# A three-stage kernel: last stage's first chunks converted inside the stage before, a reordered start, and a reordered last block

## The chip, the cores and the metric

The kernel runs on one core of a Trainium2 chip, in one launch. The metric is the device time of an execution in microseconds (us); the document compares medians over runs and reads single profiled executions. The engines are TensorE (PE; its weight loads are PEld), VectorE (DVE), ScalarE (ACT), GpSimd (POOL) and SyncE (SP), which here mainly issues the transfers (DMA).

## What is computed

Three functions are applied one after the other: attention with a decay taken from a running sum, a mixture of experts with one expert per token (MoE1), and a dense layer pair with h·cos(h) between (MoE2).

```python
# attention: q, k, v (4, 8, 576, 64), s (4, 8, 576)
cum = np.cumsum(np.maximum(s, 0.0), axis=-1)
bias = -(cum[:, :, :, None] - cum[:, :, None, :])
scores = np.where(causal, -1e9, scale * q @ k.T + np.minimum(bias, 0.0))
attn = softmax(scores); x = attn @ v              # x: 2304 tokens x 512
# MoE1: 8 experts, w1 (8, 512, 1024), w2 (8, 1024, 512)
expert_idx = argmax(xn @ en.T / tau)              # xn, en: rows over their norms
out[mask] = gate_w[mask, None] * (np.maximum(x[mask] @ w1[e], 0.0) @ w2[e])
# MoE2: w_in (512, 2048), w_out (2048, 512)
h = x @ w_in
return (h * np.cos(h)) @ w_out
```

## The kernel before

**Attention** goes through 16 pairs of heads. For a pair, `load` fetches q and k, `load_c` the running sums, `load_v` the values. A pair has four steps n: `sco` makes score products on PE, `mx` adds the decay and takes the maximum on DVE, `ex` exponentiates on ACT, `tr` transposes on PE, `av` makes the products with v. The running sums `cum` are made by a scan on DVE over 32 rows (one per head), stored to DRAM as `cumd` by a transfer that ACT issues, and fetched from there, spread over partitions, as `c_t`. For the first pair there is no time for that round trip: `first_c` makes `c_t` by products of a selecting matrix (`sel2`, or a column of the identity `idt`) with `cum`, with 32 rows, copies halves of 288 columns out with ACT and DVE, and `mask` adds the causal mask on DVE and POOL. `setup_b` to `setup_d` make the norms of the expert embeddings: one product (`n_ps`), a root on POOL in some ten small operations (`en`), its inverse on DVE (`ien`). A plan (`at(pair, where, ...)`) says at which point of which pair they stand. In attention the order on all engines is written out by hand.

**MoE1** has 72 steps (`NS`), 8 for each of nine rounds of tokens. A step makes `h_ps` (12 products, `emit_h`), takes relu and splits the result into a high part `hh` (ACT) and a rest `hl` (DVE), and, one step later, adds 12 products to four accumulators (`emit_o`). Every matrix is held as a high part and a rest, so that each product is three (high·high, high·rest, rest·high). After a round's eighth step the four accumulators become `x2h` (ACT copy) and `x2l` (DVE subtraction), the input of MoE2. `finish` writes the steps; only SP's order is by hand there, that of the other engines is made by the scheduler.

**MoE2** goes through 16 chunks of 128 hidden columns with five blocks of tokens (four of 512, one of 256). A chunk arrives in float64 in two halves of 512 columns (`wraw`; the first for `w_in`, the second for `w_out`) and `load_chunk` converts each half: four DVE operations on the bits (`cva`, `cvp`), an ACT cast to `wh`, two more DVE operations to `wl`. The conversions are tasks that `advance` moves on by one piece after each half step; `finish` begins chunks 0 to 3 in MoE1's last steps, `moe2` chunks 4 and 5 at once. In a step `emit_h` makes `h_ps` (12 products), h·cos(h) goes over ACT (`ki`), DVE, ACT (sine), DVE, then ACT (`gh`, the high part) and DVE (`gl`, the rest); `emit_o`, two steps later, adds three products for each 128 tokens to `facc`. The result is added into `oacc` by DVE and each 128 rows go out by an indirect transfer from POOL. Four h steps' results fit in PSUM.

Of the kernel before, what the change touches and what calls it, by code (L numbers as in the profile page):

```python
# [23 lines left out]
E, F = 8, 1024  # L24
# [18 lines left out]
def moe_kernel(ctx, tc, qd, kd, vd, sd, ied, embt, tau, ident, maskd, trid, wcat, wf, out):  # L43
# [9 lines left out]
    g.chunks, g.tasks, g.loading = {}, [], {}  # L53
# [11 lines left out]
    with ExitStack() as m1:  # L65
        with tc.manual_schedule(engines={ET.SP, ET.PE, ET.Activation, ET.DVE, ET.Pool}):
            attention(g, wcat, qd, kd, vd, sd, ied, embt, tau, ident, maskd, trid)
            steps, finish = moe1(g, m1, wcat, wf)
# [4 lines left out]
        with tc.manual_schedule(engines={ET.SP}):  # L73
            finish()
    with tc.manual_schedule(engines={ET.SP}):
        early.close()
        moe2(g, wf)
        st.close()
# [26 lines left out]
def attention(g, wcat, qd, kd, vd, sd, ied, embt, tau, ident, maskd, trid):  # L105
# [6 lines left out]
    with ExitStack() as st:  # L112
# [49 lines left out]
        def mask(p):  # L162
# [4 lines left out]
            if p == 0:  # L167
                nc.vector.tensor_tensor(out=tail, in0=tail, in1=mk_f[:, 128:192], op=ALU.add)
                yield
                for h in range(2):  # L170
                    nc.vector.tensor_tensor(out=c[:, h, 512:640], in0=c[:, h, 512:640], in1=mk_f[:, 0:128], op=ALU.add)
# [12 lines left out]

        s_t = sx.tile([128, S], F32, tag="sx", name="s_t")[0:B * H]
# [10 lines left out]
        cum = sx.tile([128, S], F32, tag="sx", name="cum")[0:B * H]  # L196
# [4 lines left out]
        sel2 = one.tile([B * H, 128], F32, name="sel2")  # L201
        nc.vector.tensor_copy(out=sel2.rearrange("p (a b) -> p a b", a=2), in_=idt[0:B * H, 0:2].unsqueeze(2).to_broadcast([B * H, 2, 64]))
# [11 lines left out]
        load(1)  # L214
# [6 lines left out]
        emb_t = one.tile([128, 4, E], F32, name="emb_t")  # L221
# [5 lines left out]
        ones_f = one.tile([128, 128], F32, name="ones_f")  # L227
# [15 lines left out]
        nc.gpsimd.memset(ones_f, 1.0)  # L243
# [7 lines left out]
        def setup_loads():  # L251
            nc.sync.dma_start(out=ie, in_=ied)
            nc.sync.dma_start(out=emb_t, in_=embt)
# [21 lines left out]
        def setup_a():  # L275
            nc.gpsimd.tensor_copy(out=tri_b, in_=tri_f)
            nc.gpsimd.tensor_tensor(out=sq, in0=emb_t, in1=emb_t, op=ALU.mult)
# [347 lines left out]
        at(1, "b", setup_b)  # L625
        at(2, "rb", setup_c)
        at(2, "b", setup_d)
# [40 lines left out]
        mx(2)  # L668
        ex(2)
        next(mask(1))  # L670
        mx(3)
        fills = [0, 1, 2, 3, 4, 4, 5, 5]
        for p in range(NPAIR):
# [23 lines left out]
            tr(n)  # L697
# [47 lines left out]
def moe1(g, st, wcat, wf):  # L745
# [3 lines left out]
    if True:  # L749
# [226 lines left out]
        def emit_o(n):  # L976
# [18 lines left out]
            if f == 7:  # L995
                xT.pop(r)
                off_r = offset(r)
                for d in range(4):
                    nc.scalar.copy(out=x2h[:, d, bass.ds(off_r, c)], in_=acc[d][:, 0:c])
                    nc.vector.tensor_tensor(out=x2l[:, d, bass.ds(off_r, c)], in0=acc[d][:, 0:c],  # L1000
# [35 lines left out]
        def finish():  # L1036
            split(g, load_at[8], raws.pop(load_at[8]))
            for n in range(9, NS):
                r, f = steps[n]
                if n in load_at:  # L1040
                    l = load_at[n]
                    if l < len(loads):
                        load_w(l)
                    else:
                        start_chunk(g, wf, l - len(loads))
                        advance(g.tasks)
                emit_h(n)
                emit_o(n - 1)
                advance(g.tasks)
# [11 lines left out]
        return s, finish  # L1061
# [3 lines left out]
def overlap(g, s):  # L1065
# [17 lines left out]
    r.gate_b()  # L1083
    r.place()
# [128 lines left out]
def load_chunk(g, wf, c):  # L1213

    nc = g.nc
    hi = g.ringp.tile([128, 1024], F32R, tag="wh", name="wh")
    lo = g.ringp.tile([128, 1024], F32R, tag="wl", name="wl")
# [5 lines left out]
    g.chunks[c] = (hi, lo)  # L1223
    for z, raw in enumerate(raws):
        yield
        t, p = yield from to_f32_parts(nc, g.cv, raw)
# [4 lines left out]
        nc.vector.tensor_tensor(out=lo[:, sl], in0=t, in1=p, op=ALU.add)  # L1231

# [11 lines left out]
def moe2(g, wf):  # L1244
    tc, nc, const, out = g.tc, g.nc, g.const, g.out
    with ExitStack() as st:
# [30 lines left out]
        def emit_h(n):  # L1277
# [3 lines left out]
            for _ in g.loading.pop(c, ()):  # L1281
                pass
# [8 lines left out]
            t = h_cos_h(nc, tg.tile([128, 512], I32, tag="ki", name="ki")[:, 0:w], h, hpi)  # L1291
# [101 lines left out]
```

## Times and profile before

| | us |
|---|---|
| runs | 833.91, 834.93, 834.78 |
| median | 834.78 |
| profiled execution, device time | 834.91 |
| its span, first to last instruction | 833.0 |
| PE busy | 802.2 (96%) |
| DVE busy | 569.6 (68%) |
| ACT busy | 421.9 (51%) |
| POOL busy | 139.0 (17%) |
| mean granted clock of TensorE | 0.992 |

The page gives busy times over the whole span, and attention takes about its first 165 us, MoE1 the time up to about 411, MoE2 the rest. Which engine sets the pace is read stage by stage, from the idle time in square brackets that a row of the timeline carries: how long the engine stood before that instruction and what released it. The clock that the throttle granted TensorE is given for stretches, 1.00 being 2.4 GHz and 0.50 being 1.2 GHz; the ends of matmuls are modelled, so distances between starts are used.

### The profile page before, as it was taken

How to read it: one execution, taken by the hardware profiler on the slowest of the kernel's cores; microseconds unless marked ns; L12 is line 12 of the kernel's file. 1: busy time of each engine (PE TensorE's matmuls, PEld its weight loads, DVE VectorE, ACT ScalarE, POOL GpSimd, SP SyncE). 2: the span in 40 equal slices, each digit the busy share in tenths (PEclk: the TensorE clock that was granted, in tenths of full speed). 3: DMA queues.
4: the chain of work that ended last, by engine and by line, in shares of the span. 5: the costliest groups of instructions: out<-in, count | busy, mean ns of one | idle time of the engine just before them, and what ended most of it. 6: DMA issues, size and time to landing. Idle time of an engine off the chain costs nothing. (4 is left out here: it accounts for less than half of the span.)

```text
span 833.0 us, 15110 instructions
## 1 busy us (share of the span) xinstructions
PE 802.2 (96%) x5607; PEld 666.0 (80%) x5607; DVE 569.6 (68%) x1254; ACT 421.9 (51%) x894; POOL 139.0 (17%) x274
## 2 busy tenths in 40 slices
PE   7999999999999999999989999999999999999994
PEld 4666666689999999999868888888888888888883
DVE  5879897974765565566989577775877758444462
ACT  4988888732545454555255453333433434333331
POOL 4447665340011101100000000000000000000133
PEclk9999999999999999999989999999999999999998
DMA  7999875548757689774432111110111100000122
GB/s 239 311 354 349 260 242 168 171 162 323 260 152 190 141 161 194 205 174 164 142 101 77 51 51 50 52 52 1 50 52 51 51 1 2 1 0 1 52 78 102
DMA packets 41712, 109.06 MB, mean 131 GB/s; under 512 B 7392, under 2 KB 7904, under 8 KB 41632
## 3 DMA queue, kind: packets, MB, share of 16 engines
q1 hardware_dynamic: 38032, 98.50, 39.9%
q0 software_dynamic: 3552, 9.45, 3.1%
q8 instruction: 46, 0.75, 0.4%
q14 instruction: 34, 0.28, 0.1%
q10 hardware_dynamic: 48, 0.07, 0.0%
HBM read 92.19 MB, written 15.81 MB: 130 GB/s over the span
## 5 line engine op out<-in xcount | busy, mean ns | idle before, releaser
L101 DVE TENSOR_TENSOR wl<-wraw,wh 128x1024 fp32r<-128x1024 f32 x64 | 78.2, 1224 | 66.9 <-ACT wh L99 66.8
L1287 PE MATMUL h_ps<-x2h,wh 128*128 128x512 f32 (+1 forms) x320 | 118.9, 371 | 1.1 <-DVE x2l L1000 1.1
L1307 PE MATMUL facc<-wh,gh 128*128 128x512 f32 x288 | 115.7, 402 | 3.8 <-ACT gh L1294 3.8
L1288 PE MATMUL h_ps<-x2l,wh 128*128 128x512 f32 (+1 forms) x320 | 118.4, 370 | 0.0
L1289 PE MATMUL h_ps<-x2h,wl 128*128 128x512 f32 (+1 forms) x320 | 118.3, 370 | 0.0
L1309 PE MATMUL facc<-wh,gl 128*128 128x512 f32 x288 | 114.8, 399 | 0.0
L1308 PE MATMUL facc<-wl,gh 128*128 128x512 f32 x288 | 114.7, 398 | 0.0
L1148 ACT ACTIVATE ki<-h_ps 128x512 int32<-128x512 f32 (+1 forms) x80 | 44.5, 557 | 119.9 <-PE h_ps L1289 119.4
L1149 DVE SCALAR_TENSOR_TENSOR ki<-ki,h_ps 128x512 f32<-128x512 int32 (+1 forms) x80 | 50.5, 632 | 71.4 <-ACT ki L1148 71.0
L99 ACT CAST wh<-wraw 128x1024 fp32r<-128x1024 f32 x64 | 67.1, 1050 | 52.6 <-PE acc L993 47.5
L1319 POOL DMA_INDIRECT out_dram<-oacc,ti x18 | 17.5, 971 | 439.9 <-DVE oacc L1317 436.2
L604 ACT ACTIVATE s_sb<-s_sb,mx 128x576 f32<-128x576 f32 (+2 forms) x144 | 83.0, 581 | 5.5 <-DVE mx L336 5.4
L1150 ACT ACTIVATE ki<-ki,hpi 128x512 f32<-128x512 f32 (+1 forms) x80 | 54.5, 682 | 48.3 <-DVE ki L1149 48.3
L993 PE MATMUL acc<-hl,wh 128*128 128x256 f32 (+7 forms) x256 | 76.6, 299 | 0.7 <-DVE hl L965 0.7
L992 PE MATMUL acc<-hh,wh 128*128 128x256 f32 (+7 forms) x256 | 77.3, 302 | 0.0
L994 PE MATMUL acc<-hh,wl 128*128 128x256 f32 (+7 forms) x256 | 76.4, 298 | 0.0
L1294 ACT CAST gh<-ki 128x512 fp32r<-128x512 f32 (+1 forms) x80 | 46.3, 578 | 53.1 <-DVE ki L1151 53.1
L1287 PEld LDWEIGHTS h_ps<-x2h,wh 128*128 128x128 f32 x320 | 60.1, 188 | 13.4 <-DVE x2l L1000 1.3
L1288 PEld LDWEIGHTS h_ps<-x2l,wh 128*128 128x128 f32 x320 | 60.2, 188 | 12.3 <-DVE x2l L1000 0.6
L1151 DVE TENSOR_TENSOR ki<-h_ps,ki 128x512 f32<-128x512 f32 (+1 forms) x80 | 50.7, 634 | 27.3 <-ACT ki L1150 27.3
L1289 PEld LDWEIGHTS h_ps<-x2h,wl 128*128 128x128 f32 x320 | 60.2, 188 | 11.3
L959 PE MATMUL h_ps<-xth,wh 128*128 128x368 f32 (+6 forms) x224 | 68.6, 306 | 0.0
(241 smaller groups left out, 1686.6 us busy)
## 6 DMA issues: line engine op xcount, KB each, us to landing
wraw<-in_wcat_dram SPq DMA_DIRECT2D x64, 512.0 KB, 4.8
wraw<-in_wf_dram SPq DMA_DIRECT2D x32, 512.0 KB, 3.7
k_t<-in_kd_dram SPq DMA_DIRECT2D x16, 496.0 KB, 9.8
c_t<-cumd SPq DMA_DIRECT2D x15, 512.0 KB, 6.9
xr<-zr SPq DMA_DIRECT2D x8, 768.0 KB, 9.4
xw<-xr SPq DMA_DIRECT2D x7, 768.0 KB, 8.3
q_t<-in_qd_dram SPq DMA_DIRECT2D x16, 320.0 KB, 6.6
v_t<-in_vd_dram SPq DMA_DIRECT2D x16, 320.0 KB, 7.8
```

What stands on the lines that cost most here:

```text
L101: nc.vector.tensor_tensor(out=lo, in0=raw, in1=hi.bitcast(F32), op=ALU.subtract)
L604: nc.scalar.activation(**kw)
L959: nc.tensor.matmul(out=ps[:, 0:c], lhsT=wh[:, sl], rhs=th[:, k, 0:c], start=(k == 0), stop=False)
L992: nc.tensor.matmul(out=ps[:, 0:c], lhsT=wh[:, sl], rhs=hh[:, 0:c], start=(f == 0), stop=False)
L993: nc.tensor.matmul(out=ps[:, 0:c], lhsT=wh[:, sl], rhs=hl[:, 0:c], start=False, stop=False)
L994: nc.tensor.matmul(out=ps[:, 0:c], lhsT=wl[:, sl], rhs=hh[:, 0:c], start=False, stop=(f == 7))
L1287: nc.tensor.matmul(out=ps[:, 0:w], lhsT=wh[:, sl], rhs=g.x2h[:, k, a0:a1], start=(k == 0), stop=False)
L1288: nc.tensor.matmul(out=ps[:, 0:w], lhsT=wh[:, sl], rhs=g.x2l[:, k, a0:a1], start=False, stop=False)
L1289: nc.tensor.matmul(out=ps[:, 0:w], lhsT=wl[:, sl], rhs=g.x2h[:, k, a0:a1], start=False, stop=(k == 3))
L1307: nc.tensor.matmul(out=acc[t], lhsT=gh[:, sl], rhs=wh[:, 512:1024], start=(c == s), stop=False)
L1308: nc.tensor.matmul(out=acc[t], lhsT=gh[:, sl], rhs=wl[:, 512:1024], start=False, stop=False)
L1309: nc.tensor.matmul(out=acc[t], lhsT=gl[:, sl], rhs=wh[:, 512:1024], start=False, stop=(c == e))
```

## The change

At the start: `ones_f` is filled first and nine products of it with itself (128 by 128) stand ahead of everything on PE; `cum` has 128 rows, the upper 96 zero, and the selecting products go over all 128; a tiny exponential stands first on ACT, so that its table is loaded there; the mask's and the embeddings' transfers come early, `cumd` is stored by SP and followed by `load(1)`, ahead of `load_c(1)`; `mx(0)` comes ahead of the second pair of copies, the first pair's ten transposes `tr(0)` ahead of `sco(3)`, one mask addition goes from DVE to POOL. The norms move about one pair forward in the plan. In `overlap`, behind the gate's last exponential, a tiny sine loads the sine table.

At the transition: `finish` stops four steps earlier, and `last_steps` writes MoE1's last four with SP's, ACT's and DVE's order by hand. Only chunk 0 and the first operations of chunk 1 are converted there; chunks 2, 3, 4, 5 are begun at MoE2's steps 1, 4, 8, 11. A chunk's halves are waited for apart (`half_of`). In the last block (256 tokens) the last four h steps share two buffers and come earlier; their products with `w_out` go by row tile.

```diff
         at(0, "b", setup_a)
-        at(1, "b", setup_b)
-        at(2, "rb", setup_c)
-        at(2, "b", setup_d)
+        at(0, "c", setup_b)
+        at(0, "b", setup_c)
+        at(1, "b", setup_d)
...
+        ones_f = one.tile([128, 128], F32, name="ones_f")
+        nc.gpsimd.memset(ones_f, 1.0)
...
+        nc.sync.dma_start(out=mk_f, in_=maskd)
         load(0)
-        nc.sync.dma_start(out=mk_f, in_=maskd)
+        emb_t = one.tile([128, 4, E], F32, name="emb_t")
+        nc.sync.dma_start(out=emb_t, in_=embt)
+        w_ps = bank("w_ps")
+        for _ in range(9):
+            nc.tensor.matmul(out=w_ps[:, 0:128], lhsT=ones_f, rhs=ones_f, start=True, stop=True)
+        nc.scalar.activation(out=one.tile([128, 1], F32, name="exp0"), in_=ones_f[:, 0:1], func=ACTF.Exp)
...
+        cums = sx.tile([128, S], F32, tag="sx", name="cum")
+        nc.gpsimd.memset(cums, 0.0)
+        cum = cums[0:B * H]
...
-        nc.scalar.dma_start(out=cumd, in_=cum)
+        nc.sync.dma_start(out=cumd, in_=cum)
+        load(1)
...
-            sel = sel2 if k == 2 else idt[0:B * H, k:k + 1].to_broadcast([B * H, 128])
+            sel = sel2 if k == 2 else idt[:, k:k + 1].to_broadcast([128, 128])
...
-                nc.tensor.matmul(out=ps, lhsT=sel, rhs=cum[:, c0:c0 + 288], start=True, stop=True)
+                nc.tensor.matmul(out=ps, lhsT=sel, rhs=cums[:, c0:c0 + 288], start=True, stop=True)
...
         load_c(1)
-        load(1)
...
         sco(0)
+        mx(0)
         first_c(0)
         next(m0)
-        mx(0)
         ex(0)
         first_c(1)
         sco(1)
+        sco(2)
         next(m0)
-        sco(2)
+        nc.gpsimd.tensor_tensor(out=sq, in0=emb_t, in1=emb_t, op=ALU.mult)
         mx(1)
         ex(1)
-        sco(3)
+        tr(0)
         mx(2)
         ex(2)
+        sco(3)
...
+            start_chunk(g, wf, 0)
+            advance(g.tasks)
+
+        def last_steps():
+            for n in range(NS - 4, NS):
+                if n > NS - 4:
+                    advance(g.tasks)
+                emit_h(n)
+                emit_o(n - 1)
+                if n < NS - 1:
+                    advance(g.tasks)
+                if n == NS - 2:
+                    start_chunk(g, wf, 1)
+                    g.tasks.reverse()
+                    advance(g.tasks[0:1])
+                    g.tasks.reverse()
             emit_o(NS - 1)
...
     r.gate_b()
+    g.nc.scalar.activation(out=g.count.tile([128, 1], F32, name="sin0"), in_=r.l[:, 0, 0:1], func=ACTF.Sin, scale=0.0)
...
+def half_of(g, c, z):
+
+    while c in g.loading and g.halves.get(c, 0) <= z:
+        if next(g.loading[c], 0) is not None:
+            break
...
-        for c in range(LW, RING):
-            start_chunk(g, wf, c)
         LO = 2
-        for n in range(NS):
+        begin = {1: 2, 4: 3, 8: 4, 11: 5}
+        for n in range(NS - 4):
+            if n in begin:
+                start_chunk(g, wf, begin[n])
             emit_h(n)
-            advance(g.tasks)
+            if n:
+                advance(g.tasks)
+            else:
+                with tc.issue_after(g.turned.ins):
+                    advance(g.tasks)
             if n >= LO:
                 emit_o(n - LO)
                 advance(g.tasks)
-        for n in range(NS - LO, NS):
-            emit_o(n)
+        emit_h(NS - 4)
+        emit_o(NS - 6)
+        emit_h(NS - 3)
+        emit_h(NS - 2)
+        emit_o(NS - 5)
+        emit_h(NS - 1)
+        for t, n in ((0, 4), (0, 3), (0, 2), (1, 4), (1, 3), (1, 2), (0, 1), (1, 1)):
+            emit_o(NS - n, t)
```

PE at the very start of the kernel, before (`c_ps` are the selecting products, `s_ps` scores, `t_ps` transposes):

```order
L208 MATMUL c_ps<-cum,sel_127 128x288 x2
L310 MATMUL s_ps<-k_t,q_t 64x288 x4
L208 MATMUL c_ps<-cum,idt 128x288 x4
L316 MATMUL s_ps<-k_t,q_t 128x512 x2
L316 MATMUL s_ps<-k_t,q_t 128x384 x2
L316 MATMUL s_ps<-k_t,q_t 128x256 x2
L316 MATMUL s_ps<-k_t,q_t 128x128 x2
L310 MATMUL s_ps<-k_t,q_t 64x288 x4
L352 MATMUL t_ps<-idt,s_sb 128x64 x26
```

The same place with the change:

```order
L200 MATMUL w_ps<-ones_f 128x128 x9
L221 MATMUL c_ps<-cum,sel_148 128x288 x2
L317 MATMUL s_ps<-k_t,q_t 64x288 x4
L221 MATMUL c_ps<-cum,idt 128x288 x4
L323 MATMUL s_ps<-k_t,q_t 128x512 x2
L323 MATMUL s_ps<-k_t,q_t 128x384 x2
L359 MATMUL t_ps<-idt,s_sb 128x64 x10
L323 MATMUL s_ps<-k_t,q_t 128x256 x2
L323 MATMUL s_ps<-k_t,q_t 128x128 x2
L317 MATMUL s_ps<-k_t,q_t 64x288 x4
L359 MATMUL t_ps<-idt,s_sb 128x64 x16
```

The nine products come first, and ten of the 26 transposes have moved ahead of the narrow scores.

DVE at the end of MoE1, before (`cva`, `cvp`, `wl` are conversion, `x2l` the input of MoE2):

```order
L1230 TENSOR_TENSOR cva<-cva,wh 128x512
L1000 ISA
L1000 TENSOR_TENSOR x2l<-acc_6100,x2h 128x264
L1231 TENSOR_TENSOR wl<-cva,cvp 128x512
L1000 ISA
L1000 TENSOR_TENSOR x2l<-acc_6104,x2h 128x264
L1136 TENSOR_SCALAR cva<-wraw 128x512
L1000 ISA
L1000 TENSOR_TENSOR x2l<-acc_6108,x2h 128x264
L1137 SCALAR_TENSOR_TENSOR cva<-wraw,cva 128x512
L1000 ISA
L1000 TENSOR_TENSOR x2l<-acc_6112,x2h 128x264
```

The same place with the change:

```order
L1158 TENSOR_SCALAR cva<-wraw 128x512
L1159 SCALAR_TENSOR_TENSOR cva<-wraw,cva 128x512
L975 SCALAR_TENSOR_TENSOR hl<-h_ps,hh 128x264
L830 TENSOR_LOAD pki_3502
L1010 ISA
L1010 TENSOR_TENSOR x2l<-acc_6115,x2h 128x264
L1010 ISA
L1010 TENSOR_TENSOR x2l<-acc_6119,x2h 128x264
L1010 ISA
L1010 TENSOR_TENSOR x2l<-acc_6123,x2h 128x264
L1010 ISA
L1010 TENSOR_TENSOR x2l<-acc_6127,x2h 128x264
```

The four subtractions now stand in a row, with the two last conversion operations ahead of them instead of in between.

PE at this place, MoE1's last `emit_o` (`acc` are the four accumulators), before:

```order
L992 MATMUL acc_6100<-hh,wh 128x264
L993 MATMUL acc_6100<-hl,wh 128x264
L994 MATMUL acc_6100<-hh,wl 128x264
L992 MATMUL acc_6104<-hh,wh 128x264
L993 MATMUL acc_6104<-hl,wh 128x264
L994 MATMUL acc_6104<-hh,wl 128x264
```

The same place with the change:

```order
L1002 MATMUL acc_6115<-hh,wh 128x264
L1002 MATMUL acc_6119<-hh,wh 128x264
L1002 MATMUL acc_6123<-hh,wh 128x264
L1002 MATMUL acc_6127<-hh,wh 128x264
L1003 MATMUL acc_6115<-hl,wh 128x264
L1004 MATMUL acc_6115<-hh,wl 128x264
L1003 MATMUL acc_6119<-hl,wh 128x264
L1004 MATMUL acc_6119<-hh,wl 128x264
```

The four products of the high part now come ahead of the first one that needs `hl`.

ACT from the last copy to `x2h` on, before (`ki` alternates between the rounding and the sine of h·cos(h)):

```order
L999 COPY x2h<-acc_6112 128x264
L1228 CAST wh<-cva 128x512 x2
L1148 ACTIVATE ki<-h_ps 128x512
L1150 ACT_TABLE_LOAD
L1150 ACTIVATE ki<-ki,hpi 128x512
L1148 ACTIVATE ki<-h_ps 128x512
L1228 CAST wh<-cva 128x512
L1294 CAST gh<-ki 128x512
```

The same place with the change:

```order
L1009 COPY x2h<-acc_6127 128x264
L1170 ACTIVATE ki<-h_ps 128x512
L1252 CAST wh<-cva 128x512
L1172 ACTIVATE ki<-ki,hpi 128x512
L1170 ACTIVATE ki<-h_ps 128x512
L1327 CAST gh<-ki 128x512
L1172 ACTIVATE ki<-ki,hpi 128x512
```

The table load and two casts are gone from the row, and the cast to `gh` comes one sooner behind the first sine.

## Rows read from the trace of the kernel before

**Rows 1.** Waits of TensorE, whole run: waited for, us in total, times, longest

```profile
PE facc L1307 <- ACT gh L1294: 3.8, 1, 3.8
PE h_ps L950 <- ACT x L921: 1.4, 1, 1.4
```

**Rows 2.** Three stretches: busy us (x instructions) per engine, PEclk, DMA share, GB/s

```profile
6.00:7.00 1.00, 1.00 (x7) 0.24 (x9) 0.00 (x0) 0.63 (x2) 0.00 (x0) 1.00 0.00 0
426.00:428.00 2.00, 2.00 (x7) 1.51 (x6) 2.00 (x4) 0.32 (x1) 0.00 (x0) 0.50 0.25 102
500.00:600.00 100.00, 100.00 (x456) 81.89 (x455) 72.70 (x126) 40.70 (x68) 0.00 (x0) 1.00 0.13 43
```

**Rows 3.** Timeline, PE, start and one steady pair: start us, us, engine, line, op

```profile
4.70 2.28 PE L208 MATMUL c_ps<-cum,sel 32*128 32x288 f32 x4 [4.70 <-DVE sel L202]
...
6.91 1.24 PE L310 MATMUL s_ps<-k_t,q_t 64*64 64x288 f32 x8
...
8.07 4.20 PE L208 MATMUL c_ps<-cum,idt 32*128 32x288 f32 x8
...
12.21 3.36 PE L316 MATMUL s_ps<-k_t,q_t 64*128 64x512 f32 x8
...
26.93 1.72 PE L316 MATMUL s_ps<-k_t,q_t 64*128 64x512 f32 x8
```

**Rows 4.** Timeline, other engines at the start

```profile
0.71 0.53 POOL L240 MEMSET zr<- 128x512 f32 x1 [0.29 <-POOLq L1385]
...
4.95 1.28 ACT L211 ACT_TABLE_LOAD   x1 [4.95 <-DVE sel L202]
...
14.44 0.69 DVE L336 CUSTOM_DVE_ANT_0 s_sb<-s_ps,c_t 128x512 f32<-128x512 f32 x1 [1.41 <-PE s_ps L316]
```

**Rows 5.** Timeline, fourth pair: DVE waits for a chain on POOL, PE for DVE

```profile
43.72 0.20 DVE L291 RECIPROCAL ien<-en 128x8 f32<-128x8 f32 x1 [2.24 <-POOL en L288]
...
44.27 0.71 PE L352 MATMUL t_ps<-idt,s_sb 64*128 64x64 f32 x15 [0.79 <-DVE ot L690]
```

**Rows 6.** Timeline, PE, end of the first MoE and start of the second

```profile
409.64 0.39 PE L993 MATMUL acc<-hl,wh 128*128 128x264 f32 x1 [0.67 <-DVE hl L965]
...
412.38 0.50 PE L1287 MATMUL h_ps<-x2h,wh 128*128 128x512 f32 x1 [1.12 <-DVE x2l L1000]
...
415.50 0.39 PE L1287 MATMUL h_ps<-x2h,wh 128*128 128x512 f32 x1
...
421.03 0.40 PE L1287 MATMUL h_ps<-x2h,wh 128*128 128x512 f32 x1
...
425.24 0.79 PE L1307 MATMUL facc<-wh,gh 128*128 128x512 f32 x1 [3.81 <-ACT gh L1294]
...
431.18 0.39 PE L1287 MATMUL h_ps<-x2h,wh 128*128 128x512 f32 x1
```

**Rows 7.** Timeline, DVE, same place: conversion's first operation twice, then splits

```profile
400.79 0.43 DVE L1136 TENSOR_SCALAR cva<-wraw 128x512 uint32<-128x512 uint32 x1 [1.08 <-DMA wraw<-in_wf_dram]
...
404.90 0.43 DVE L1136 TENSOR_SCALAR cva<-wraw 128x512 uint32<-128x512 uint32 x1
...
409.16 0.43 DVE L965 SCALAR_TENSOR_TENSOR hl<-h_ps,hh 128x264 fp32r<-128x264 f32 x1
...
411.89 0.43 DVE L1000 TENSOR_TENSOR x2l<-acc,x2h 128x264 f32 x1
```

**Rows 8.** Timeline, ACT: behind the last gate exponential, and at the transition

```profile
180.85 0.39 ACT L964 ACTIVATE hh<-h_ps 128x256 fp32r<-128x256 f32 x1 [1.29 <-PE h_ps L961]
...
410.75 1.21 ACT L999 CAST x2h<-acc 128x264 f32 x4
...
419.62 1.28 ACT L1150 ACT_TABLE_LOAD   x1
```

**Rows 9.** Page, busy tenths of DMA in 40 equal slices of the span

```profile
DMA  7999875548757689774432111110111100000122
```

**Rows 10.** Page, DMA issues: xcount, KB each, median us from issue to landing

```profile
wraw<-in_wf_dram SPq DMA_DIRECT2D x32, 512.0 KB, 3.7
```

More of the change, by code (lines that the diff above doesn't have):

```diff
@@ L52, in moe_kernel @@
     g.tc, g.nc, g.const, g.dram, g.xr, g.out = tc, nc, const, dram, xr, out
-    g.chunks, g.tasks, g.loading = {}, [], {}
+    g.chunks, g.tasks, g.loading, g.halves = {}, [], {}, {}
     ET = mybir.EngineType
@@ L74, in moe_kernel @@
             finish()
+        with tc.manual_schedule(engines={ET.SP, ET.Activation, ET.DVE}):
+            last_steps()
     with tc.manual_schedule(engines={ET.SP}):
@@ L999, in emit_o @@
                     nc.scalar.copy(out=x2h[:, d, bass.ds(off_r, c)], in_=acc[d][:, 0:c])
-                    nc.vector.tensor_tensor(out=x2l[:, d, bass.ds(off_r, c)], in0=acc[d][:, 0:c],
+                    g.turned = nc.vector.tensor_tensor(out=x2l[:, d, bass.ds(off_r, c)], in0=acc[d][:, 0:c],
                                             in1=x2h[:, d, bass.ds(off_r, c)].bitcast(F32), op=ALU.subtract)
@@ L1037, in finish @@
             split(g, load_at[8], raws.pop(load_at[8]))
-            for n in range(9, NS):
+            for n in range(9, NS - 4):
                 r, f = steps[n]
                 if n in load_at:
[L1041 to L1045, printed above, removed]
-                        advance(g.tasks)
+                    load_w(load_at[n])
                 emit_h(n)
                 emit_o(n - 1)
-                advance(g.tasks)
                 if f == 3 and r + 1 < E:
@@ L1222, in load_chunk @@
         raws.append(raw)
-    g.chunks[c] = (hi, lo)
     for z, raw in enumerate(raws):
         yield
+        if not z:
+            hi = g.ringp.tile([128, 1024], F32R, tag="wh", name="wh")
+            lo = g.ringp.tile([128, 1024], F32R, tag="wl", name="wl")
+            g.chunks[c] = (hi, lo)
+            g.halves[c] = 0
         t, p = yield from to_f32_parts(nc, g.cv, raw)
@@ L1280, in emit_h @@
             w = a1 - a0
-            for _ in g.loading.pop(c, ()):
-                pass
+            half_of(g, c, 0)
             wh, wl = ring[c]
@@ L1290, in emit_h, with emit_o @@
             h = ps[:, 0:w]
-            t = h_cos_h(nc, tg.tile([128, 512], I32, tag="ki", name="ki")[:, 0:w], h, hpi)
-            gh = gp.tile([128, 512], F32R, tag="gh", name="gh")
-            gl = gp.tile([128, 512], F32R, tag="gl", name="gl")
-            nc.scalar.copy(out=gh[:, 0:w], in_=t)
-            nc.vector.tensor_tensor(out=gl[:, 0:w], in0=t, in1=gh[:, 0:w].bitcast(F32), op=ALU.subtract)
+            k = n - (NS - 4)
+            if k < 0 or k % 2 == 0:
+                gs["t"] = [p.tile([128, 512], d, tag=q, name=q) for p, d, q in ((tg, I32, "ki"), (gp, F32R, "gh"), (gp, F32R, "gl"))]
+            t, gh, gl = (a[:, 256 * (k % 2):256 * (k % 2) + w] if k >= 0 else a[:, 0:w] for a in gs["t"])
+            t = h_cos_h(nc, t, h, hpi)
+            nc.scalar.copy(out=gh, in_=t)
+            nc.vector.tensor_tensor(out=gl, in0=t, in1=gh.bitcast(F32), op=ALU.subtract)
             gs[n] = (gh, gl)
-        def emit_o(n):
+        def emit_o(n, only=None):
             tb, c, s, e = steps[n]
             a0, a1 = blocks[tb]
+            half_of(g, c, 1)
             wh, wl = ring[c]
-            gh, gl = gs.pop(n)
-            for t in range((a1 - a0) // 128):
+            gh, gl = gs[n]
+            tiles = range((a1 - a0) // 128) if only is None else (only,)
+            for t in tiles:
                 if c == s:
@@ L1310, in emit_o @@
             if c == e:
-                for t in range((a1 - a0) // 128):
+                for t in tiles:
                     i = a0 // 128 + t
@@ L1322, in emit_o @@
                         sent.append(ins.ins)
-            if n == last[c]:
+            if n == last[c] and only is None:
                 start_chunk(g, wf, c + RING)
-        for c in range(LW, RING):
-            start_chunk(g, wf, c)
         LO = 2
-        for n in range(NS):
+        begin = {1: 2, 4: 3, 8: 4, 11: 5}
+        for n in range(NS - 4):
+            if n in begin:
+                start_chunk(g, wf, begin[n])
             emit_h(n)
-            advance(g.tasks)
+            if n:
[3 more added lines that the diff above has]
+                    advance(g.tasks)
             if n >= LO:
```

22 lines of the change are left out of this document (8 added, 14 removed).

## The prediction

> **What bounds the kernel now.** The waits of TensorE come first: over the whole run it waits for others in a dozen places, the longest inside the program being 3.8 us, and the longest that the change leaves alone 1.4 us [rows 1]. The stretches come second: from 500 to 600 us PE is busy in every microsecond at a granted clock of 1.00 [rows 2], and the view of PE's waits from 432 to 822 us is empty. So PE is the bound nearly everywhere, and a gain can only come from where PE stands still or runs at half clock. Three such places are left, and the timeline shows each: the start, one stall in the fourth pair, and the step from MoE1 to MoE2. A fourth candidate, the end, is ruled out below.
>
> **The start.** PE's first matmul is at 4.70, when the scan and the selecting matrix are ready [rows 3]. The forms that follow run at half speed: the eight score products that begin at 12.21 last 3.36 us, while the same eight in the third pair last 1.72 [rows 3], a ratio of 1.95. (PEclk reads 1.00 there; I trust the durations.) From 4.70 to the maximum at 14.44, which waited 1.41 us for PE [rows 4], the chain is 2.21 (first `c_ps`), 1.16 (scores), 4.14 (four `c_ps`) and 2.23 us (wide scores and their way to DVE), 9.74 in all. The change puts nine products of ones in PE's idle 4.7 us. *Their price:* four `c_ps` products take 4.14 us, so one of 288 columns takes 1.03, one of 128 columns 0.46, and nine 4.1 us; from about 1 us on (an estimate: POOL's first filling starts at 0.71 [rows 4], and `ones_f` is now that first one) they end near 5.1, and the first `c_ps` is 0.4 us late. *What they may buy* depends on when the clock rises, which this trace shows once for certain: at the transition PE resumes at 425.24 and is at full pace at 431.18 [rows 6], 5.9 us later. I take the same distance, so a rise at 6.9. Then the first `c_ps` ends at about 7.1, the remaining 1.16 + 4.14 + 2.23 = 7.53 us shrink by 1.95 to 3.9, and the maximum comes at 11.0 instead of 14.44. I take off 0.2 for the copies and masks of DVE, ACT and POOL, which now follow each other more closely: **3.2 us**. Bounds: a rise at once would bring 9.74 × (1 − 1/1.95) = 4.7, less 0.3 for k's transfer, which has only landed by 6 (DMA share 0.00 from 6 to 7 [rows 2]), so 4.4; no rise before 18 brings nothing and costs the 0.4.
>
> The other edits there serve this gain. ACT's table load of 1.28 us, up to 6.24 [rows 4], is done before its copy; in the old trace it hardly mattered, in the new one it would hold the copy. `cumd` is stored by SP, and on that queue `load(1)`, the fetches of `c_t`, `load_v` and the rest stand behind the wait for the scan; they waited for `cumd`'s landing before, so nothing is later, and the second pair's q and k fill the microsecond in which DMA moved nothing [rows 2]. Transfers thus start some 2.5 us sooner, nearly what the earlier PE asks of them. Going from 32 to 128 rows changes no duration that I charge: a product's time goes with its columns.
>
> **The clock's rule.** In the rows, PE was busy almost without pause from 4.70 to 12.21 and was still at half speed after that [rows 3]. The Trainium skill ("TensorE: Matmul & The Clock Gate", Part 1) says that the clock follows how busy PE was recently and that its window does not restart with the kernel. Plain busyness would have lifted the clock well before 12.21, so the trace doesn't bear the rule out as it stands; by the rule the nine products lift it, without it nothing says that they do. That is the first rival.
>
> **The fourth pair.** PE stands 0.79 us at 44.27, behind a DVE that waited 2.24 us for the last of POOL's root operations [rows 5]. The change makes the norms about one pair, some 8 us, earlier, which ends this stall; the norm's products and POOL operations are as many as before. I take **0.7** (bounds 0 and 0.9: DMA is busy to the full from the second to the fourth fortieth of the span, 21 to 83 us [rows 9], and a pair that runs faster may then wait for its k).
>
> **The transition, what is lost.** PE waits 0.67 us for `hl` at 409.64, 1.12 us for `x2l` at 412.38 and 3.81 us for `gh` at 425.24 [rows 6]. The pace of a 512-column matmul is (421.03 − 415.50) / 24 = 0.2304 us [rows 6]. From 412.38 to 431.18 PE starts 51 of them (37 up to 421.03, 14 from 425.24 on), which at that pace is 11.75 us; it took 18.80, so 7.05 are lost: 0.36 in the first step, 3.98 idle before 425.24, and 2.71 because 14 matmuls then ran at the granted clock of 0.50 [rows 2, 6]. With 0.67 and 1.12 that makes **8.84 us**. The reason is DVE: the conversion of one half takes 404.90 − 400.79 = 4.1 us with one `hl` inside [rows 7], so 3.8 alone and 7.6 a chunk, and four chunks are being converted around this place, in front of `hl`, `x2l` and the first h·cos(h); beside that, ACT loads the sine's table at 419.62 for 1.28 us [rows 8].
>
> **The transition, what stays.** Only one and a half chunks are left to convert there. *`hl`:* in the new order it still stands behind conversion operations and comes as late as 409.16 [rows 7]; three more products of the high part (3 × 0.12) go ahead of it, so 0.3 of 0.67 stay. *`x2l`:* the copy of the first accumulator (0.4, from 1.21 for four [rows 8]) and the subtraction (0.43 [rows 7]) must follow that accumulator's last product, and six products of the others (0.7) now lie beside them; with the hand-over 0.5 stay of 1.12. *First h·cos(h):* the first step's `h_ps` is done 2.9 us after MoE2 starts on PE, its `gl` is asked for 36 × 0.23 = 8.3 us after that start. Between them lie ACT 0.6, DVE 0.6, ACT 0.7, DVE 0.6, ACT 0.6 and DVE 0.6 us, 3.7 together, and about 3 us of conversion and second-step work in the way on DVE: due at 9 rather than 8.3, but PE's first two products need only `gh`, so 0.2 stay. No idle time of several microseconds is left, so the clock stays up and the 2.71 go as well. 8.84 − 1.0 = **7.8 us**; bounds 8.8, and 6.0 if each of the three waits is some 0.6 longer.
>
> *What the move costs:* chunks 2 to 5 are converted later, during MoE2. A step there has 24 matmuls, 5.5 us of PE, and asks 1.8 us of DVE for the gate; chunk 2, begun at step 1 and used at step 5, has four steps, 22 us less 7, in which 3.8 us of chunk 1 and 7.6 of its own fit. That cover holds 3.6 us of slack. Its transfers take 3.7 us from issue to landing [rows 10]. The sine table load lands behind the last gate exponential, where ACT stood 1.29 us before its next `hh` at 180.85 [rows 8]; by the row's 1.28 us it costs nothing. The Trainium skill ("ScalarE: Activation LUTs", "What ACT_TABLE_LOAD costs") adds a drain to the load, 2.66 us in all for a switch; by that `hh` would be up to 1.4 us late and the time 824.5, but no row here shows ACT idle behind a load.
>
> **The end.** PE reaches its last matmul without idle time, and the two last row tiles are finished in the same order as before. Moving the last h steps changes no wait that exists: 0, bounds −0.3 and +0.3.
>
> **The sum.** 3.2 + 0.7 + 7.8 = 11.7 us. The profiled execution took 834.91, so 823.2; it lies 0.13 above the median of the runs, 834.78, so the forecast is **823.1**. Best ends of all terms: 4.4 + 0.9 + 8.8 + 0.3 = 14.4, 820.4.
>
> **The rivals.** *A, the clock does not rise early.* For it: early busy work didn't lift it in the old trace. Against: the new products use all 128 rows, as the matmuls at 425.24 did, the old ones 32 or 64 [rows 3]. The start then costs 0.2 to 0.4 instead of giving 3.2: 826.6. *B, the stall moves on once.* One chunk half or gate of MoE2's first steps is late by some 4 us, PE idles and falls to half clock again: 3.98 + 2.71 = 6.7 us return: 829.8. For it: the slack of 3.6 us in DVE's cover is my own sum. Against: ACT and DVE no longer convert ahead. *C, slower.* The same at several of the four late beginnings (chunks 2 to 5): each late chunk costs 6.7, so two give 13.4, more than the 11.7 gained: 836.5; it decides from the second late chunk. Against: later chunks have more steps each. *D, the change does not do what it says:* the scheduler or the transfers keep DVE as full as before and the clock stays low at the start: about 834.5.
>
> **Chances.** Forecast 0.67 (821 to 825), A 0.14, B 0.10, C 0.03, D 0.03, better than 820 0.03. The range reaches past A and stops short of B: 820.0 to 828.5. 0.2% is 1.7 us, about what a measurement of this kernel can tell from no change: faster 0.94, same 0.03, slower 0.03.
>
> **What would show it.** The profile after should have the maximum of step 1 near 11 us and the 512-column score products at 1.7 us; no idle time near 41 us; at the transition no PE idle time above 0.6 us, PEclk 1.00 throughout and no table load; MoE2's matmuls at 0.230 us without a gap. A first score row of 3.4 us would mean A; a PEclk of 0.50 after 400 us, B or C. The forecast fails if DMA, full up to 83 us, makes PE wait for k or v.

## The result, and the profile after

The changed kernel takes 825.46 us in the median of its four runs (822.98 to 826.72), the kernel before 834.86; the ratio is 0.9884, with a 95% interval from 0.9857 to 0.991. The gain is 9.4 us where 11.7 were forecast, so the time lies 2.4 us above the forecast of 823.1: inside the range, but above the 821 to 825 to which the forecast gave its own chance of 0.67. The fastest run, 822.98, is at the forecast. Why the others are not is the main question of what follows.

The profiled execution took 826.06 us, span 824.3. First its matmuls at the start (timeline, PE; columns as in [rows 3]; each product here stands as two records, so nine products are x18) and the maximum that followed the wide scores (DVE):

```profile
0.97 4.21 PE L200 MATMUL w_ps<-ones_f 128*128 128x128 f32 x18 [0.97 <-POOL ones_f L188]
...
4.97 1.97 PE L221 MATMUL c_ps<-cum,sel 128*128 128x288 f32 x4
...
6.88 0.72 PE L317 MATMUL s_ps<-k_t,q_t 64*64 64x288 f32 x8
...
7.52 2.21 PE L221 MATMUL c_ps<-cum,idt 128*128 128x288 f32 x8
...
9.66 1.77 PE L323 MATMUL s_ps<-k_t,q_t 64*128 64x512 f32 x8
```

```profile
10.93 0.69 DVE L343 CUSTOM_DVE_ANT_0 s_sb<-s_ps,c_t 128x512 f32<-128x512 f32 x1 [0.78 <-PE s_ps L323]
```

Against [rows 3] the nine products fill the first 5 us, the first `c_ps` is 0.27 later, the scores behind it take 0.72 instead of 1.24, the four `c_ps` 2.21 instead of 4.20, the eight records of wide scores 1.77 instead of 3.36, and the maximum comes at 10.93 instead of 14.44 [rows 4]: the clock is up before 7 us.

Then the waits of TensorE over the whole run (columns as in [rows 1]); what was there before and is gone is 3.8 us for `gh`, 0.7 for `hl`, 0.8 in the fourth pair, and most of the 1.1 for `x2l`:

```profile
PE rk_ps L482 <- DVE oh_all L472: 2.3, 3, 1.8
...
PE s_ps L317 <- DMA k_t<-in_kd_dram: 0.4, 1, 0.4
...
PE h_ps L1318 <- DVE x2l L1010: 0.2, 1, 0.2
```

New are 1.8 us (of the first line's 2.3) for `oh_all`, the choice of the expert, and 0.4 for k; smaller ones are 0.9 more for `mx`, 0.7 more for MoE1's `h` and 0.5 for `pt`. The first matmul of MoE2, and two stretches (columns as in [rows 2]), the first around the place where the clock had been at 0.50 [rows 2]:

```profile
409.35 0.50 PE L1318 MATMUL h_ps<-x2h,wh 128*128 128x512 f32 x1 [0.21 <-DVE x2l L1010]
```

```profile
410.00:430.00 20.00, 20.00 (x88) 16.12 (x87) 19.62 (x35) 11.98 (x21) 0.00 (x0) 1.00 0.25 86
500.00:600.00 100.00, 100.00 (x454) 81.67 (x453) 72.92 (x126) 40.19 (x68) 0.00 (x0) 1.00 0.12 42
```

PE is busy in every microsecond from 410 to 430 at a granted clock of 1.00: the old stall of 3.81 us and the half clock behind it [rows 6] are gone. Setting starts of the same work side by side gives the ledger of the two profiled executions:

| the same work in both | before | after | difference |
|---|---|---|---|
| scores of the third pair | 25.42 | 22.55 | −2.87 |
| scores of the fourth pair | 34.33 | 30.96 | −3.37 |
| scores of the sixth pair | 51.10 | 46.84 | −4.26 |
| scores of the seventh pair | 61.86 | 57.60 | −4.26 |
| scores of the eighth pair | 71.16 | 69.91 | −1.25 |
| scores of the sixteenth pair | 147.43 | 146.44 | −0.99 |
| MoE1's last output step | 408.69 | 407.18 | −1.51 |
| rounding (`ki`) of MoE2's fourth step | 433.53 | 423.67 | −9.86 |
| last matmul | 821.31 | 812.56 | −8.75 |

Up to the third pair's scores the changed kernel has already made the norm's products (0.99 us from start to start), which the old one makes just behind them, so the start is worth 2.87 + 0.99 = 3.9. Of these 0.5 go by the fourth pair (0.43 of it waiting for k), 0.89 come from the stall of [rows 5], and **3.0 are lost between the scores of the seventh and the eighth pair**. Another 0.26 go by the sixteenth pair, and 0.52 come back by MoE1's last step; what made these two isn't known. The transition then brings 9.86 − 1.51 = 8.35. The last 1.1 go over MoE2: PE starts 454 matmuls in 100 us, against 456 in [rows 2], without any wait. That is a difference of pace between executions, not of the kernel: of the runs below, `m_sin_only` with the old step to MoE2 shows 454 and `m_no_sin` with the new one 455 and 456.

The loss of 3.0 in detail, on POOL, DVE and PE, and the clock behind it:

```profile
57.90 0.32 POOL L179 TENSOR_TENSOR c_t<-c_t,mk_f 128x64 f32<-128x64 f32 x1 [5.67 <-DMA c_t<-cumd]
...
62.74 0.27 POOL L459 TENSOR_TENSOR l<-lg,ien 128x40 f32<-128x40 f32 x1
```

```profile
63.04 0.20 DVE L465 TENSOR_REDUCE lm<-l 128x5 f32<-128x40 f32 x1 [1.39 <-POOL l L459]
...
64.24 0.06 DVE L472 MEMSET oh_all<- 64x4 uint32 x1
```

```profile
64.44 0.18 PE L482 MATMUL rk_ps<-oh_all,tri_b 128*128 128x40 bf16 x1 [1.81 <-DVE oh_all L472]
...
64.94 3.79 PE L384 MATMUL o_ps<-pt,v_t 128*64 128x320 f32 x20 [0.19 <-DVE pt L620]
```

```profile
62.00:64.00 2.00, 0.63 (x8) 0.39 (x5) 0.82 (x5) 1.51 (x5) 1.67 (x5) 1.00 1.04 270
65.00:67.00 2.00, 2.00 (x8) 0.94 (x10) 1.91 (x9) 1.48 (x5) 1.03 (x6) 0.50 1.05 388
```

POOL works in order. The mask of the eighth pair's `c_t` stands on it ahead of the gate's small operations of the sixth pair (`lw`, `lg`, `l`). It waited 5.67 us for its transfer, which landed near 57.9; its five operations take 3 us, the gate's follow, `l` at 62.74, and with it DVE's choice (`lm` to `oh_all`) and PE's `rk_ps` at 64.44. PE stood 1.81 us, and the 20 output products behind it took 3.79 us instead of the usual 2.27, because the granted clock had fallen to 0.50. DMA was full (share 1.04 to 1.05).

### The profile page after: what moved, and what is told of

Read it like the earlier page. It is cut to its first block, busy times and chain, and to the rows that moved or that the text cites. A ratio compares the mean times of both kernels' runs of the same rounds, so it can differ in the third digit from the quotient of the medians.

```text
span 824.3 us, 15146 instructions
## 1 busy us (share of the span) xinstructions
PE 800.7 (97%) x5625; PEld 666.6 (81%) x5625; DVE 569.5 (69%) x1253; ACT 422.9 (51%) x896; POOL 140.6 (17%) x276
```

## Experiments

Every run is compared with runs of the kernel before on the same chip; chips differ (its median was 834.41, 837.34 and 834.09 in the three sets), so differences between sets are taken by the ratio.

**Is it this loss, and does it repeat?** The changed kernel once more:

> The changed kernel once more, on the same chip as the three below. Theory 1 (the start's gain is given back in the sixth pair: POOL, which works in order, waits for a transfer of c_t that comes late because DMA is full, the gate's operations queue behind it, PE idles about 1.9 us and falls to half clock, some 3 us in all): about 825.5 us, and the profile again shows PE waiting about 1.8 us for oh_all near 64 us. Theory 2 (an accident of one execution): 823 us and no such wait.

It took 823.28 us (822.78 to 825.34), ratio 0.9865 (0.9845 to 0.9884). In its profile the mask started at 57.72, `oh_all` was ready at 64.10 and PE waited as well, but for about half as long, and the clock stayed up:

```profile
64.25 0.18 PE L482 MATMUL rk_ps<-oh_all,tri_b 128*128 128x40 bf16 x1 [0.98 <-ACT s_sb L611]
...
64.75 2.27 PE L384 MATMUL o_ps<-pt,v_t 128*64 128x320 f32 x20 [0.19 <-DVE pt L620]
```

The row names ACT as what ended PE's wait, but `oh_all` was only just ready, and the choice on DVE had waited 0.56 us for `l` on POOL: it is the same chain. So neither expectation was met in full: the wait repeats, its size and the half clock do not. Here the seventh pair took 68.19 − 58.25 = 9.94 us, against 12.31 in the profile above and 9.30 before. Whether this loss is what spreads the runs over 823 to 827 us is not shown: only two executions have a trace, and this one took 825.34 us, the slowest of its five, with 0.64 us lost here.

**The mask behind the gate's operations** (eighth pair's mask only):

```diff
+        at(5, "m", lambda: next(mask(7)))
...
-            if p % 4 == 0 and 0 < p < NPAIR - 3:
+            if p % 4 == 0 and 4 < p < NPAIR - 3:
```

> The changed kernel with one move: the mask of the eighth pair's c_t is issued on POOL behind the gate's operations of the sixth pair instead of ahead of them. Theory 1: the wait of 1.8 us and the half clock at 64 us go, 3 us less than the changed kernel, about 822.5 us. Rival: DMA, full until 83 us, is the limit itself, so that PE waits elsewhere (for the mask, for k or v) and the time stays within 0.5 us of the changed kernel.

822.29 us (821.91 to 822.78), ratio 0.9852 (0.9833 to 0.987); a second time, in the third set, 823.05 us, ratio 0.9857 (0.9803 to 0.9912):

> The kernel mask7 once more, as the measure for the three beside it on this chip: 12 us below the kernel before, runs within 1 us of each other.

There the runs spread over 2.9 us (821.89 to 824.76) rather than 1; what moved them isn't known. In the profile of the first, `l` is on POOL 3.3 us sooner, the mask comes behind it, and PE is at full clock where it had been at 0.50:

```profile
59.48 0.26 POOL L459 TENSOR_TENSOR l<-lg,ien 128x40 f32<-128x40 f32 x1
...
63.02 0.32 POOL L179 TENSOR_TENSOR c_t<-c_t,mk_f 128x64 f32<-128x64 f32 x1
```

```profile
65.00:67.00 2.00, 2.00 (x26) 1.08 (x23) 1.90 (x13) 1.97 (x9) 1.77 (x6) 1.00 1.05 405
```

The seventh pair takes 66.20 − 56.90 = 9.30 us, as before the change. The transfer itself is as late as it was: 9.0 us from SP's issue to its landing, 8.9 in the changed kernel. By the medians the kernel is 1.0 us below the changed one on the same chip, not the 3 us of theory 1, and the intervals of the two ratios overlap: 3.0 us is what one execution lost, not what the median run loses.

**Why the transfer is late: the load on DMA.** The changed kernel, mask not moved, with two of the eight zero fills of MoE1's token buffer (768 KB each) later:

```diff
-        fills = [0, 1, 2, 3, 4, 4, 5, 5]
+        fills = [0, 1, 4, 4, 4, 4, 5, 5]
```

> The changed kernel (mask not moved) with the two zero fills of the third and fourth pairs issued in the fifth, behind its c_t: DMA then has 1.6 MB less to move ahead of the c_t that POOL waits for. If that transfer's lateness is what starts the loss of the sixth pair: POOL gets it some 4 us sooner, before 55 us, and PE's wait for oh_all near 64 us shrinks to 0.3 us; the time, 822 to 824, depends on what the later fills then delay. If DMA's load is not the cause: the mask starts at 57 to 58 us and PE waits as in the changed kernel.

822.49 us (822.06 to 823.27), ratio 0.9847 (0.9793 to 0.9901). POOL has the transfer 5 us sooner (2.2 of them because SP issues it sooner, 2.9 because it lands 6.0 us after its issue instead of 8.9), and PE's wait at this place is down to 0.33:

```profile
52.67 0.32 POOL L179 TENSOR_TENSOR c_t<-c_t,mk_f 128x64 f32<-128x64 f32 x1 [2.53 <-DMA c_t<-cumd]
```

```profile
62.45 0.18 PE L482 MATMUL rk_ps<-oh_all,tri_b 128*128 128x40 bf16 x1 [0.33 <-POOL rd L278]
```

Two edits that have nothing in common but this chain, one on POOL's order and one on DMA's load, take the loss away. It is not an accident of one execution: in all eight profiles with the mask moved, those of the runs below included, PE waits 0.33 us here, and from the third to the sixteenth pair's scores seven of them take 120.46 or 120.47 us (`m_no_sin` 120.89). `fills` takes 120.48, the changed kernel 123.89 and 121.98. The chain is shown: full DMA, late `c_t`, POOL in order, gate, PE. By the ratios the two kernels, 0.9852 (or 0.9857) and 0.9847, cannot be told apart.

**The two halves of the change apart.** Attention's edits alone, and all others alone:

> The kernel before with the edits of attention alone (products of ones, order of the start, transfers, norms); the step from MoE1 to MoE2 as before. Theory 1: the start gains about 4, the fourth pair 0.9, and some 3.5 are given back up to 70 us: 833.3 us, 1.5 less than before. Rival (the start's gain reaches the end and the transition gains less than it seems): 830.5 us.

> The kernel before with the other edits alone: sine table early, MoE1's last steps by hand, chunks begun late, last block's order. Theory 1: the transition's waits and half clock are worth 8.3 us whatever attention does: 826.5 us. Rival: 829 us or more, if half the gain came from the attention's earlier end.

Attention alone: 832.77 us, ratio 0.9984 (0.9969 to 1.0), with runs from 830.78 to 836.86. Its profiled run is the fastest of them, and there the seventh pair takes 9.29 us and the gain at the sixteenth pair is 4.3, though the mask had not been moved. So the median met the first expectation, but the reason that it gave is not seen: the one execution with a trace gives nothing back, and what made the slow ones slow is open. The others alone: 826.45 us (825.46 to 826.95), ratio 0.9901 (0.9884 to 0.9918), as expected, 8.0 us with attention as it was. Of the two, the transition is the sure part. Singly the halves bring 1.6 and 8.0 us, together 11.1 on the same chip (834.41 − 823.28); the 1.5 between is about what the intervals allow, and no run explains it.

**What lifts the clock at the start.** Three kernels with `mask7` as their base: without the nine products; with the products over 32 rows; with the selecting products over 32 rows again.

```diff
-        for _ in range(9):
-            nc.tensor.matmul(out=w_ps[:, 0:128], lhsT=ones_f, rhs=ones_f, start=True, stop=True)
```

```diff
-            nc.tensor.matmul(out=w_ps[:, 0:128], lhsT=ones_f, rhs=ones_f, start=True, stop=True)
+            nc.tensor.matmul(out=w_ps[:, 0:128], lhsT=ones_f[0:32], rhs=ones_f[0:32], start=True, stop=True)
```

```diff
-            sel = sel2 if k == 2 else idt[:, k:k + 1].to_broadcast([128, 128])
+            sel = sel2[0:B * H] if k == 2 else idt[0:B * H, k:k + 1].to_broadcast([B * H, 128])
...
-                nc.tensor.matmul(out=ps, lhsT=sel, rhs=cums[:, c0:c0 + 288], start=True, stop=True)
+                nc.tensor.matmul(out=ps, lhsT=sel, rhs=cum[:, c0:c0 + 288], start=True, stop=True)
```

> The kernel mask7 without the nine products of ones, all else kept. If the products lift the clock (my theory): the first eight wide score products take 3.4 us again, the maximum of step 1 comes near 13.8, and the time is 3.3 us above mask7, about 825.6 us. Rival (the other edits of the start bring it: 128 rows, order of the transfers, table load): wide scores at 1.8 us, time within 0.6 us of mask7, 822.3 to 822.9.

> The kernel mask7 with the nine products of ones over 32 rows instead of 128, so that TensorE is as long busy ahead of the first selecting product. If being busy is enough to lift the clock: as mask7, 822.3 us, wide scores at 1.8 us. If rows count (early work on 32 and 64 rows did not lift it in the kernel before): wide scores slow, 824 to 825.6 us, as without the products.

> The kernel mask7 with the selecting products over 32 rows again, the nine products of ones kept on 128. If the products of ones alone lift the clock: as mask7, 822.3 us. If 128 rows are needed after them: wide scores at 3.4 us and 824 to 825.6 us.

Times: 826.18 us, ratio 0.9869 (0.9853 to 0.9886); 827.70, 0.9889 (0.9872 to 0.9905); 826.79, 0.9891 (0.9863 to 0.9919). By the ratio that is 1.4, 3.1 and 3.3 us above `mask7` (0.9852), with wide intervals. But `mask7` itself did not run in this set, and in all four profiles of the set (these three and `m_no_sin` below) PE takes 15.13 to 15.17 us from the sixteenth pair's scores to that pair's output products, in all ten others 13.99 to 14.01. That 1.1 us is there whatever the edit; whether the kernel before has it on this chip too, so that the ratio takes it out, isn't known. Beside `m_no_sin`, which has the whole start and took 826.22 us in the same set, the three lie 0.0, 1.5 and 0.6 us higher. So the times do not settle what each edit costs; the traces, one for each kernel, tell more. Without the products:

```profile
4.77 2.26 PE L218 MATMUL c_ps<-cum,sel 128*128 128x288 f32 x4 [4.77 <-POOL rs L391]
...
6.96 1.24 PE L314 MATMUL s_ps<-k_t,q_t 64*64 64x288 f32 x8
...
8.13 2.46 PE L218 MATMUL c_ps<-cum,idt 128*128 128x288 f32 x8
...
10.52 1.77 PE L320 MATMUL s_ps<-k_t,q_t 64*128 64x512 f32 x8
```

With the products over 32 rows:

```profile
0.97 4.20 PE L200 MATMUL w_ps<-ones_f 32*128 32x128 f32 x18 [0.97 <-POOL ones_f L188]
...
5.10 2.29 PE L221 MATMUL c_ps<-cum,sel 128*128 128x288 f32 x4
...
8.49 3.11 PE L221 MATMUL c_ps<-cum,idt 128*128 128x288 f32 x8
...
11.54 1.77 PE L323 MATMUL s_ps<-k_t,q_t 64*128 64x512 f32 x8
```

With the selecting products over 32 rows:

```profile
5.11 1.64 PE L221 MATMUL c_ps<-cum,sel 32*128 32x288 f32 x4
...
7.33 2.22 PE L221 MATMUL c_ps<-cum,idt 32*128 32x288 f32 x8
...
9.48 3.36 PE L323 MATMUL s_ps<-k_t,q_t 64*128 64x512 f32 x8
```

The form behind the tile names gives the rows (32\*128 or 128\*128). Nine products over 32 rows keep PE just as busy, 4.2 us without a pause, but what follows runs at half clock (2.29 and, partly, 3.11 us, against 1.97 and 2.21 in the changed kernel); the clock is up for the wide scores, 1.77 us, so the second expectation for this run was met in the cause but not in these scores. Behind nine products over 128 rows the clock is up before the first `c_ps` end (1.64 us, then 2.22, in the third kernel). But there it falls again behind 4.4 us of products over 32 rows and, for the narrow scores, 64 (5.11 to 9.48): the wide scores take 3.36 us, with PE busy throughout. And without any products the clock rises behind the selecting ones over 128 rows, somewhat later: 2.46 for the four `c_ps`, 1.77 for the wide scores. Products over 64 rows do not let it fall in the steady pairs: in `mask7` PE makes nothing else from 46.14 to 51.20 us, at full pace. The maximum that came at 14.44 before [rows 4] comes at 11.79 without products, at 12.81 with products of 32 rows, at 11.70 with selecting products of 32 rows, and at 10.56 to 11.27 in the nine profiles with the whole start (10.68 in `mask7`). So the nine products are worth 0.5 to 1.2 us. The 128 rows of the selecting products make most of the rest: without the nine products PE's work up to the wide scores differs from that of the kernel before in these rows alone, and the maximum comes 2.65 us sooner. The expectation of 3.3 us for the products alone was wrong.

**What made the old stall at the transition.** `mask7` without the early sine, and the kernel before with attention's edits, the moved mask and the early sine but the old step to MoE2 (and the old last block):

```diff
-    g.nc.scalar.activation(out=g.count.tile([128, 1], F32, name="sin0"), in_=r.l[:, 0, 0:1], func=ACTF.Sin, scale=0.0)
```

> The kernel mask7 without the early sine, so that the table is loaded at the first sine of MoE2 again. My theory (the conversions in front of the gate made most of the old stall, the load only its own 1.28 us): the first gl is 1.3 us later than in mask7, PE waits about 1 us once, the clock stays up: 823.3 us. Rival (the load made the stall): PE waits over 3 us and falls to half clock, 826 us or more.

> The kernel before with the start's edits, the moved mask and the early sine, but with the step from MoE1 to MoE2 as before (four chunks converted ahead). My theory (DVE's conversions in front of the gate make the old stall, and the half clock with it): PE waits some 2.5 to 3.8 us for gh at the first output products, the clock falls, and the kernel is 4.2 to 6 us below the kernel before, 6 to 8 above mask7. Rival (the table load makes it): no wait above 1 us, within 2 us of mask7.

The first took 826.22 us, ratio 0.9870 (0.9853 to 0.9887), by the ratio 1.5 above `mask7`. That is the rival's time (826 us or more) without the rival's wait, and at most 0.6 us of it lie at this step: MoE2 starts 4.4 us later than in `mask7` (409.93 for 405.53), and from there to the fourth step's rounding it takes 14.95 us instead of 14.35, to the end of the span 414.5 instead of 415.3. What attention and MoE1 lose in this run isn't the sine's. The load stands where it stood before, and PE waits 0.28 us for `gh`, with the clock up:

```profile
415.14 1.28 ACT L1172 ACT_TABLE_LOAD   x1
```

```profile
418.82 0.51 PE L1342 MATMUL facc<-wh,gh 128*128 128x512 f32 x1 [0.28 <-ACT gh L1327]
```

The second took 829.11 us (827.33 to 831.06), ratio 0.9927 (0.9898 to 0.9955), 6.1 above `mask7` beside it. With the table long loaded PE still waits 2.82 us, and the clock falls:

```profile
418.67 0.51 PE L1317 MATMUL facc<-wh,gh 128*128 128x512 f32 x1 [2.82 <-ACT gh L1304]
```

```profile
419.00:421.00 2.00, 1.92 (x6) 1.21 (x5) 2.00 (x4) 1.67 (x4) 0.00 (x0) 0.63 0.00 0
421.00:423.00 2.00, 2.00 (x6) 1.60 (x5) 1.60 (x4) 1.50 (x4) 0.00 (x0) 0.51 0.62 193
```

So the conversions in front of the gate made some 6 of the 8 us, and about 1 us of the old idle time of 3.81 [rows 6] was the table load's; attention alone, with the old step and the load in it, shows the 3.81 as well. From MoE2's first matmul to the end of the span the three profiles with the old step take 419.3 to 420.6 us, the eleven with the new one 414.5 to 415.3. This runs as the prediction had it.

**The end.** `mask7` with the last block in the order of the kernel before:

```diff
-        emit_h(NS - 4)
-        emit_o(NS - 6)
...
-            emit_o(NS - n, t)
+        for n in range(NS - 4, NS):
+            emit_h(n)
+            emit_o(n - LO)
+        for n in range(NS - LO, NS):
+            emit_o(n)
```

> The kernel mask7 with the last block's steps in the order of the kernel before. My theory (no wait stood there): within 0.3 us of mask7. Rival (the new order hides the last gate): 0.5 to 2 us slower.

823.38 us (821.97 to 824.99), ratio 0.9855 (0.98 to 0.9911), against 823.05 for `mask7` beside it: no difference that these runs can tell, and no wait of PE from 430 to 822 us in either. The new order of the last block brings nothing measurable.

## Why the prediction came out as it did

**The bound.** That PE was the bound nearly everywhere, and that a gain could only come from three places, held. All three gained, in the sizes 3.9, 0.89 and 8.35 for 3.2, 0.7 and 7.8.

**The start: the size right, the cause half right.** The maximum came at 10.93 for 11.0, and the first `c_ps` was 0.27 late for 0.4. The rise of the clock, taken to be at 6.9 from one distance at the transition, came somewhat sooner: the first `c_ps` take 1.14 to 1.97 us in the nine profiles with the whole start, less than the 2.28 of half clock in all of them. In six of the nine PE then waited 0.27 to 0.59 us for k, for which the prediction had 0.3 only in its bounds. That 11.0 fits so well is in part luck. The step "Going from 32 to 128 rows changes no duration that I charge" holds for a product's own time (2.22 us over 32 rows, 2.21 over 128) and missed what mattered: the rows that PE's products had used went with the clock's rise and with its staying up. The prediction named them against rival A but put no term on them. With the nine products alone, without the 128 rows after them, the wide scores took 3.36 us. Rival A, no early rise, is out. With nine products over 32 rows PE was busy without a pause from 0.97 us on, and the `c_ps` at 8.49 still ran partly at half pace. The rule of the Trainium skill ("TensorE: Matmul & The Clock Gate", Part 1) that the clock follows how busy PE was, held against the trace in the prediction, does not by itself account for this run.

**The fourth pair and DMA: the step that was mis-sized.** The stall went (0.89), in part by luck: in the run of the other edits alone, whose attention is the old one, it isn't there either. The mask that stands ahead of the root on POOL started at 36.41 in the kernel before, behind a wait of 5.49 us for its `c_t`, and at 34.96 in that run; DVE then waited 0.81 us for the root instead of 2.24, and PE not at all. So the old stall, too, hung on a late `c_t`. The prediction saw the danger, "a pair that runs faster may then wait for its k", but bounded it by the 0.9 us of this one term, as if a full DMA could take back no more than what the norms had won. In the profiled execution it took back 0.5 (most of it for k) and 3.0 us of the start's gain. What was not followed is the queue: a pair that asks for its data sooner than DMA can bring it does not wait at its own scores but wherever an engine that works in order meets the late transfer first, here POOL, with another pair's gate behind it. How far the mask stands from the scores of the seventh pair, which PE makes just ahead of `rk_ps`, decides (SP's second issue of the eighth pair's `c_t`, the mask's start and the scores, from the timelines):

| profile | SP issues | mask starts | scores start | mask ahead of them | PE waits |
|---|---|---|---|---|---|
| before | 51.78 | 60.34 | 61.86 | 1.52 | 0.24 |
| attention alone | 46.46 | 55.66 | 57.20 | 1.54 | 0.33 |
| after, again | 48.66 | 57.72 | 58.25 | 0.53 | 0.98 |
| after | 48.23 | 57.90 | 57.60 | −0.30 | 1.81 |

A delay of 1.8 us from the first row to the last makes 1.57 more waiting; 1.1 of it is the longer time from issue to mask (9.67 for 8.56 us; in the first two rows the mask waited for DVE's `mx`, not for the transfer, so that 8.56 is only an upper bound of the transfer's time there). With two fills later that time is 6.6 (46.06 to 52.67). The half clock behind the longest of these waits made another 1.5 us of it.

**The transition.** Waits of 0.3, 0.5 and 0.2 us were left for `hl`, `x2l` and `gl`; there are one of 0.21 for `x2l` and none above 0.2 for the other two. DVE kept up with the four chunks begun late; rivals B, C and D found nothing here. The sine's table load stands behind the gate's last exponential and delays a cast there by some 1.5 us; PE shows no wait for it:

```profile
177.10 1.28 ACT L1105 ACT_TABLE_LOAD   x1
...
178.39 0.20 ACT L1105 ACTIVATE sin<-l 128x1 f32<-128x1 f32 x1
...
178.50 1.04 ACT L101 CAST wh<-wraw 128x1024 fp32r<-128x1024 f32 x1
```

The load began 0.02 us after the exponential's end, and the sine 0.01 us after the load's. The drain that the Trainium skill ("ScalarE: Activation LUTs", "What ACT_TABLE_LOAD costs") adds to a switch does not show here; the measured 1.28 us decides.

**The end.** 0, as forecast.

**The sum.** 3.9 + 0.9 + 8.35 would have been 13.1; 3.2 were lost up to MoE2 (0.5, 3.0 and 0.26, less 0.52 that came back on the way), and 1.1 by the pace of this execution, which leaves 8.75. So the forecast was near because terms erred against each other: each place gave more than was put down, and attention under a full DMA took back more than the sum had left for it. The moved mask brings the time to 822.3 on one chip and 823.05 on another, close to the forecast, with DMA as full as it was.

## What to carry to other kernels

When a stage runs faster while DMA is full in it, do not look for the new wait at the consumer of the transfer alone: list what else stands behind each instruction that waits for a transfer on an engine that works in order, and put what is urgent ahead of what may be late. A short idle time of PE costs more than its length where the clock falls behind it. Filler work for the clock is to be tried in the form that it will have: here it helped over 128 rows and not over 32, and what stood between it and the work that was to gain mattered as much.

## What the hardware showed that was not expected

- The granted clock did not go with PE's being busy alone but with the rows that its products had used: 4.2 us of products over 32 rows left the clock at half, behind the same over 128 rows it rose, and behind 4.4 us of products over 32 and 64 rows it fell again while PE had no pause (wide scores 3.36 us instead of 1.77). The two cases with 32 rows are one profile each.
- A wait of 1.81 us was followed by a granted clock of 0.50 for over 3 us in one execution (20 output products 3.79 instead of 2.27 us); one of 0.98 us at the same place in another was not. In the sixteenth pair waits of some 0.9 and 1.03 us stand in four profiles, and in one of the four, `m_no_ones`, 20 output products then took 3.86 us.
- MoE2's matmuls without any wait came at 454 to 456 in 100 us from execution to execution, which is some 1 to 2 us over the whole stage.
